# Six of 32 softmax tiles from ScalarE to VectorE: exponential from integer bits, summed in three terms by the PV matmuls

## The chip, the cores and the metric

The kernel runs on one core of a Trainium2 chip. The metric is device time in microseconds; every figure called a time is the median of several executions. The engines are called by their names or by the profile's short forms: PE is TensorE (PEld its weight loads), ACT is ScalarE, DVE is VectorE, POOL is GpSimd, SP issues most DMAs. "Clock" is the share of TensorE's full clock that was granted.

## The reference

```python
x = A_x                                        # 1 x 2048 x 512, bf16
xn = layernorm(x)
out = x + attention(xn, wqkv, wo) + mixer(xn, w1, b1, w2, b2)

def attention(x, wqkv, wo):                    # H = 32 heads, Dh = 16
    q, k, v = split(x @ wqkv)
    p = softmax(q @ k.T * Dh ** -0.5)          # 32 heads of 2048 x 2048
    return (p @ v) @ wo

def mixer(x, w1, b1, w2, b2):                  # an MLP over the 2048 tokens, F = 1376
    h = layernorm(x)
    return (gelu(h^T @ w1 + b1) @ w2 + b2)^T
```

There are 32 x 2048 x 2048 exponentials, 134 million. That is what makes this kernel a ScalarE kernel: in its trace ScalarE is busy 97% of the span, 946.2 of 953.8 us with them.

## The kernel before

The attention is cut into 32 blocks (four query blocks of 512 by eight groups of four heads). A block has 16 "periods", one for each 128 keys. In a period PE makes the scores of four heads (four matmuls of K = 32, in four row strips of the array), ScalarE turns them into exponentials as two tiles of 128 x 1024, and two periods later PE multiplies them with V (four matmuls in four column strips, 0.40 us for the four, accumulating in one PSUM bank for the whole block). V has a column of ones, so its 17th output row is the softmax denominator. Scores have three slots of two PSUM banks each.

```python
def pslot(n):                                   # tile n uses slot n % 3
    return n % 2 if n < 2 * NKT else n % 3

def score_group(g, rs=(0, 1, 2, 3)):
    ...
    for r in rs:
        n = 2 * g + r // 2
        bk = 2 * pslot(n) + (r % 2)
        matmul(bank(bk), lhsT=KT[32*r:32*r+32, T, 128*kt:128*(kt+1)],
               rhs=QT[32*r:32*r+32, slot_q, :], tile_position=(32*r, 0))

def exp_pair(n):
    activation(pT[:, n % NPB, :], ps[:, s_*1024:(s_+1)*1024], ACTF.Exp, scale=0.25)

def pv_group(g):
    ...
    for r in range(4):                          # accumulates over kt = 0..15
        matmul(bank(PV_BANK)[32*r:32*r+32, :], lhsT=V17[:, off:off+32],
               rhs=pT[:, buf, 512*(r%2):512*(r%2+1)], tile_position=(0, 32*r))

def task_epilogue_rest(b):                      # DVE: denominators, 4 reciprocals of 128x128
    stream_shuffle(denb, OT32, [16] * 32)
    for c in range(4): reciprocal(denb[:, cs], denb[:, cs])
    gpsimd.tensor_tensor(oT, OT32, denb, mult)
```

The main loop fixes the order in which every engine gets its instructions; each engine has its own list, and the timelines show it worked through in order (in e9_inter, which has another order on PE, a PV pass starts at 782.37 us, between the score pairs at 782.05 and 782.70). In a period PE gets the four score matmuls, the PV matmuls that are due, and then up to two "side" matmuls (projections of later blocks, the MLP, the output projection), which share one bank:

```python
while True:                                     # one turn is one period
    ...
    score_group(period); exp_pair(2*period); exp_pair(2*period + 1)
    pv_group(period - LAG)                      # when due; block end: epilogue
    ...                                         # side work: at most EXTRA_BUDGET = 2 matmuls
```

The softmax here doesn't subtract the row's maximum and nothing guards it: scores larger than these inputs give would overflow.

Of the kernel before, what the change touches and what calls it, by code (L numbers as in the profile page):

```python
# [9 lines left out]
BF16 = mybir.dt.bfloat16  # L10
F32 = mybir.dt.float32
# [3 lines left out]
H = 32  # L15
# [7 lines left out]
NKT = 16  # L23
# [5 lines left out]
DEBUG_SCHED = False  # L29
LAG = 2  # L30
NPB = 10
NQS = 3
EXTRA_BUDGET = 2.0
NW1 = 2
# [150 lines left out]
def bass_parallel_sum__softmax_full_mha__mixer_token_mlp__prompt_kernel(  # L185
# [18 lines left out]
    with ExitStack() as es:  # L204
# [23 lines left out]
        pT = sb("pT", [128, NPB, 1024], BF16)  # L228
        OT32 = sb("OT32", [128, 2, 512], F32)
# [4 lines left out]
        w2blk = sb("w2blk", [128, NW2, NFT, 128], BF16)  # L234
# [5 lines left out]
        stats = sb("stats", [128, 2 * NT, 6], F32)  # L240
        mv = sb("mv", [128, 2 * NT, 4], F32)
# [3 lines left out]
        osb = sb("osb", [128, 2, 512], BF16)  # L245
        ps = es.enter_context(nc.psum_tensor("ps", [128, 8 * 512], F32))
# [37 lines left out]
        sc.add("dve", lambda e: e.memset(v17_main[:, :, 16:17], 1.0), writes=[("Vone",)])  # L284

        sc.add("pool", lambda e: e.memset(qmask[:, 0:1], 0.0), writes=[("qmask",)])
        for r in range(4):
            sc.add("pool", lambda e, r=r: e.memset(qmask[32 * r:32 * r + 16, 0:1], 1.0),
                   reads=[("qmask",)], writes=[("qmask",)])
        sc.add("pool", lambda e: e.tensor_scalar(qmask[:, 1:2], qmask[:, 0:1], -1.0, 1.0, ALU.mult, ALU.add),  # L290
# [46 lines left out]
        def ln_stats(t, which):  # L337
            src = x_sb if which == 0 else xn_sb
            skey = ("x", t) if which == 0 else ("xn", t)
            i = which * NT + t  # L340
            sc.add("dve", lambda e: e.bn_stats(stats[:, i, :], src[:, t, :]),  # L341
                   reads=[skey], writes=[("stats", i)])
            sc.add("dve", lambda e: e.bn_aggr(mv[:, i, 0:2], stats[:, i, :]),
                   reads=[("stats", i)], writes=[("mv", i)])
            sc.add("pool", lambda e: e.tensor_scalar(mv[:, i, 1:2], mv[:, i, 1:2], EPS, None, ALU.add),
                   reads=[("mv", i)], writes=[("mv", i)])
            sc.add("pool", lambda e: e.tensor_tensor(mv[:, i, 2:3], mv[:, i, 1:2], mhalf[:], ALU.pow),  # L347
                   reads=[("mv", i), ("mhalf",)], writes=[("mv", i)])

        def ln_norm(t, which):  # L350
            src = x_sb if which == 0 else xn_sb
            dst = xn_sb if which == 0 else h_sb
            skey = ("x", t) if which == 0 else ("xn", t)
            dkey = ("xn", t) if which == 0 else ("h", t)
            i = which * NT + t
            sc.add("dve", lambda e: e.tensor_scalar(dst[:, t, :], src[:, t, :], mv[:, i, 0:1], mv[:, i, 2:3],
                                                    ALU.subtract, ALU.mult),
                   reads=[skey, ("mv", i)], writes=[dkey])

        def ln_tile(t, which):  # L360
            ln_stats(t, which)
            ln_norm(t, which)
# [88 lines left out]
        def vT_evac(tiles, T, bk, evac_eng):  # L451
            n = len(tiles)
            t0_ = tiles[0]
            assert tiles == list(range(t0_, t0_ + n))
            dst = V17[:, t0_ * H * 17:(t0_ + n) * H * 17].rearrange("p (t h c) -> p t h c", t=n, c=17)[:, :, 8 * T:8 * T + 8, 0:16]
            src = bank(bk)[:, 0:128 * n].rearrange("p (t h d) -> p t h d", t=n, d=16)
            evac(evac_eng, dst, src, reads=[("bank", bk)], writes=[("V", t, T) for t in tiles])

# [14 lines left out]
        def pro_stage(s_, pre):  # L473
# [24 lines left out]
            if 0 <= t < NT and (t < NPRE + 2 or not pre):  # L498
                ln_stats(t, 0)
            t = s_ - 1  # L500
            if 0 <= t < NT and (t < NPRE + 2 or not pre):
                ln_norm(t, 0)
# [25 lines left out]
        def pro_stage_late(s_):  # L528
# [17 lines left out]
            if NPRE + 2 <= t < NT:  # L546
                ln_stats(t, 0)
            t = s_ - 1
            if NPRE + 2 <= t < NT:
                ln_norm(t, 0)  # L550

        def task_ln2():
            for t in range(NT):
                yield 0.0
                ln_stats(t, 1)
                yield 0.0
                ln_norm(t, 1)
                yield 0.0
# [32 lines left out]
        def task_w2_load(st):  # L591
# [3 lines left out]
                reads=[], writes=[("w2blk", slot)], name="ld_w2a")  # L595
            dma("sp", w2blk[0:F - 128 * (NFT - 1), slot, NFT - 1, :],
                B_w2[128 * (NFT - 1):F, 128 * st:128 * (st + 1)],
                reads=[], writes=[("w2blk", slot)], name="ld_w2b")
# [28 lines left out]
        def task_yt(st):  # L627
            slot = st % NW2
            for ft in range(NFT):
# [5 lines left out]
                    reads=[("w2blk", slot), ("gT", ft)], writes=[("bank", EX_BANK)])  # L635
# [27 lines left out]
        def final_store(st, bk):  # L663
            ob = st % 2
            sc.add("dve", lambda e: e.tensor_tensor(osb[:, ob, :], bank(bk), resid[:, st, :], ALU.add),  # L665
# [25 lines left out]
        def task_epilogue_rest(b):  # L691
            qb, G = divmod(b, NG)
            eb = b % 2
            yield 0.0
            sc.add("dve", lambda e: e.stream_shuffle(denb[:, eb, :], OT32[:, eb, :], [16] * 32),  # L695
                   reads=[("OT32", eb)], writes=[("denb", eb, c) for c in range(4)])
            for c in range(4):
                cs = slice(128 * c, 128 * (c + 1))
                yield 0.0
                sc.add("dve", lambda e, cs=cs: e.reciprocal(denb[:, eb, cs], denb[:, eb, cs]),  # L700
                       reads=[("denb", eb, c)], writes=[("denb", eb, c)])
            yield 0.0
            sc.add("pool", lambda e: e.tensor_tensor(oT[:, qb % 2, G, :], OT32[:, eb, :], denb[:, eb, :], ALU.mult),  # L703
                   reads=[("OT32", eb)] + [("denb", eb, c) for c in range(4)],
# [49 lines left out]
        def exp_pair(n):  # L754
            s_ = pslot(n)
            buf = n % NPB
            sc.add("act", lambda e: e.activation(pT[:, buf, :], ps[:, s_ * 1024:(s_ + 1) * 1024], ACTF.Exp, scale=0.25),  # L757
                   reads=[("bank", 2 * s_), ("bank", 2 * s_ + 1)], writes=[("pT", buf)], name="exp")

        def pv_group(g):  # L760
            b, kt, qb, G, T, e_ = blk_of(g)
            for r in range(4):
                n = 2 * g + r // 2
                buf = n % NPB
                h = 8 * T + 2 * r + e_
                off = (kt * H + h) * 17
                sc.add("pe", lambda e, r=r, buf=buf, off=off: e.matmul(  # L767
                    bank(PV_BANK)[32 * r:32 * r + 32, :], lhsT=V17[:, off:off + 32],
                    rhs=pT[:, buf, 512 * (r % 2):512 * (r % 2 + 1)],
                    start=(kt == 0), stop=(kt == NKT - 1), tile_position=(0, 32 * r)),  # L770
                    reads=[("V", kt, T), ("pT", buf), ("Vone",)] + (
                        [("V", kt, T + 1)] if T < 3 else ([("V", kt + 1, 0)] if kt + 1 < NKT else [("Vpad",)])),
                    writes=[("bank", PV_BANK)], name="pv")
# [16 lines left out]
        for ft in range(NFT):  # L790
            sched_list.append((P(4, 2) + 6 * ft, 2, "ut", ft))
        for st in range(NT):
            sched_list.append((P(4, 2) + 6 * NFT + 7 * st, 3, "yt", st))
        for qb in range(NQB):
            for sti in range(4):
                if qb < NQB - 1:
                    sched_list.append((P(8 * (qb + 1) + 6, 2) + 4 * sti, 0, "op", (qb, sti)))
                else:
                    sched_list.append((P(NBLK - 2, 8) + 5 * sti, 4, "op", (qb, sti)))
# [33 lines left out]
        END = NGRP + LAG + 1  # L833
        while True:
# [9 lines left out]
            if period == P(7, 0):  # L844
                for st in range(min(NW2, NT)):
                    task_w2_load(st)
                w2_loaded = min(NW2, NT)
            if period < NKT:
                score_group(period, (0, 1))
                exp_pair(2 * period)  # L850
                score_group(period, (2, 3))
                exp_pair(2 * period + 1)
            elif period < NGRP:
                score_group(period)
                exp_pair(2 * period)
                exp_pair(2 * period + 1)
            for gp in (period - LAG - 1, period - LAG):
                if not (0 <= gp < NGRP):
                    continue
                b, kt = divmod(gp, NKT)  # L860
                due = gp + LAG + (1 if (kt == 0 and b > 0) else 0)
                if due != period:
                    continue
                pv_group(gp)
                if kt == NKT - 1:
                    if b == NBLK - 1:
                        assert sl_idx >= len(sched_list) and not any(tk.kind == "op" for tk in bank_q), \
                            "pre-accumulation of the last q block must be complete before the tail"
                        tail_epilogue(b)
                    else:  # L870
                        epilogue_copy(b)
                        free_tasks.append(Task("epi", b, task_epilogue_rest(b)))
# [14 lines left out]
            while bank_q:  # L887
                tk = bank_q[0]
                if tk.req is None:
                    bank_q.pop(0)  # L890
                    if DEBUG_SCHED:
                        print("period", period, "blk", period // NKT, "done", tk.kind, tk.arg)
                    if tk.kind == "ut" and w1_loaded < NFT:
                        task_w1_load(w1_loaded)
                        w1_loaded += 1
                    if tk.kind == "yt" and w2_loaded < NT:
# [82 lines left out]
```

## Time and profile before

| | before |
|---|---|
| time, median | 983.94 us (3 runs, 980.77 to 985.01) |
| span of the profiled run | 979.6 us |
| ScalarE busy | 953.8 us (97%) |
| of that in 1024 exponentials | 946.2 us |
| steady distance from start to start of two exponentials | 903 ns |
| VectorE busy | 306.4 us (31%) |
| TensorE: mean clock | 0.81 |

The first lines of the page of the kernel before give each engine's busy time, share of the span and number of instructions; in the row of the clock each digit is one of 40 slices of the span, in tenths of the full clock.

```profile
PE 822.8 (84%) x5019; PEld 208.2 (21%) x5084; DVE 306.4 (31%) x522; ACT 953.8 (97%) x1045; POOL 70.1 (7%) x110
...
PEclk9999859988878888999999999555955555555797
```

PE looks nearly as busy as ACT, but its matmul ends are modelled, and part of its time is pacing by the exponentials. The chain of waits of the same kernel (shares of the span, by engine and then by line) says who is followed:

```profile
ACT 87%; PE 10%; DVE 2%; issue 1%; DMA 1%; ACTq 0%; SPq 0%; DVEq 0%
ACT pT L757 86%; PE ps L748 3%; PE ps L767 2%; PE ps L605 1%; PE ps L425 1%; DMA x_sb<-in_A_x_dram 1%; ACT ga_sb L620 1%; PE ps L389 0%; PE ps L407 0%; DVE denb L717 0%; PE ps L652 0%; DVE QT L438 0%; PE ps L445 0%; DVE osb L665 0%; DVE sta
```

The groups of instructions of the kernel before show what fills ScalarE, and that PE's score matmuls (line 748) sat 102.1 us waiting for the exponentials (line 757) that free their PSUM slots. The columns are line, engine, operation, tiles, shapes and count, then busy time, mean duration of one, and the idle time before, with its cause.

```profile
L757 ACT ACTIVATE pT<-ps 128x1024 bf16<-128x1024 f32 x1024 | 946.2, 1390 | 4.2 <-PE ps L748 2.6
L748 PE MATMUL ps<-QT,KT 32*128 32x512 bf16 x2048 | 448.9, 464 | 123.5 <-ACT pT L757 102.1
...
L700 DVE RECIPROCAL denb<-denb 128x128 f32<-128x128 f32 x124 | 108.8, 920 | 0.9
```

The mean duration of 1390 ns is no cost: neighbouring activations overlap. What counts is the distance from start to start in the trace: 903 ns at the median, and also at its 25th and 75th percentile. One stretch of the timeline of the kernel before (start, length, what) has 34 exponentials in 31.8 us without a gap:

```profile
start us, us, engine line op out<-in xcount [idle before <-releaser]
854.20 31.81 ACT L757 ACTIVATE pT<-ps 128x1024 bf16<-128x1024 f32 x34
```

### The profile page before, as it was taken

What the parts mean: (1) busy time and instruction counts of PE and PEld (TensorE: products, weight loads), DVE (VectorE), ACT (ScalarE), POOL (GpSimd) and SP (SyncE); (2) the same over time, 40 slices, a digit from 0 to 9 for tenths busy, and PEclk for the clock granted to TensorE, in tenths of its full rate; (3) what the DMA queues carried; (4) which work ended last, traced back from release to release, by engine and by line L of the source; (5) the groups of instructions that cost most, each with busy time, mean ns of one, the idle gap of its engine ahead of it and who ended that gap; (6) DMA issues with size and microseconds to landing.
All of it is one profiled execution on the core that took longest, in us unless ns stands there. A gap on an engine that the chain in (4) does not pass through costs nothing.

```text
span 979.6 us, 11965 instructions
## 1 busy us (share of the span) xinstructions
PE 822.8 (84%) x5019; PEld 208.2 (21%) x5084; DVE 306.4 (31%) x522; ACT 953.8 (97%) x1045; POOL 70.1 (7%) x110
## 2 busy tenths in 40 slices
PE   5888898787888878888888888989889898998885
PEld 3422213211111112222222222111211111111121
DVE  6666633234322343222333223122211212102233
ACT  5999999999999999999999999999999999999995
POOL 3213200000000000000000000000000000000000
PEclk9999859988878888999999999555955555555797
DMA  8000000122111100111011010000000000000000
GB/s 193 2 1 17 6 1 2 22 51 43 21 22 22 22 17 1 30 28 27 11 30 44 17 42 2 0 1 4 19 1 1 1 1 0 1 1 1 11 11 22
DMA packets 57013, 18.34 MB, mean 19 GB/s; under 512 B 50816, under 2 KB 56960, under 8 KB 56960
## 3 DMA queue, kind: packets, MB, share of 16 engines
q1 hardware_dynamic: 53792, 16.00, 7.1%
q10 hardware_dynamic: 3168, 1.57, 0.6%
q8 instruction: 40, 0.66, 0.3%
q14 instruction: 13, 0.11, 0.0%
HBM read 15.47 MB, written 2.10 MB: 18 GB/s over the span
## 4 chain that ended last, share of the span: by engine, by line
ACT 87%; PE 10%; DVE 2%; issue 1%; DMA 1%; ACTq 0%; SPq 0%; DVEq 0%
ACT pT L757 86%; PE ps L748 3%; PE ps L767 2%; PE ps L605 1%; PE ps L425 1%; DMA x_sb<-in_A_x_dram 1%; ACT ga_sb L620 1%; PE ps L389 0%; PE ps L407 0%; DVE denb L717 0%; PE ps L652 0%; DVE QT L438 0%; PE ps L445 0%; DVE osb L665 0%; DVE stats L341 0%
## 5 line engine op out<-in xcount | busy, mean ns | idle before, releaser
L757 ACT ACTIVATE pT<-ps 128x1024 bf16<-128x1024 f32 x1024 | 946.2, 1390 | 4.2 <-PE ps L748 2.6
L748 PE MATMUL ps<-QT,KT 32*128 32x512 bf16 x2048 | 448.9, 464 | 123.5 <-ACT pT L757 102.1
L767 PE MATMUL ps<-pT,V 128*32 128x512 bf16 x2048 | 240.3, 469 | 0.6 <-ACT pT L757 0.6
L748 PEld LDWEIGHTS ps<-QT,KT 32*128 32x128 bf16 x2048 | 95.3, 94 | 505.8 <-ACT pT L757 481.5
L688 DVE COPY OT<-ps 128x512 f32<-128x512 f32 x31 | 21.4, 692 | 322.0 <-PE ps L767 322.0
L700 DVE RECIPROCAL denb<-denb 128x128 f32<-128x128 f32 x124 | 108.8, 920 | 0.9
L703 POOL TENSOR_TENSOR oT<-OT,denb 128x512 bf16<-128x512 f32 x31 | 39.3, 1266 | 791.3 <-DVE denb L700 791.3
L767 PEld LDWEIGHTS ps<-pT,V 128*32 128x32 bf16 x2048 | 51.9, 97 | 148.1 <-issue 145.8
L605 PE MATMUL ps<-big,w1blk 128*128 128x512 bf16 (+1 forms) x158 | 54.5, 419 | 6.5 <-issue 3.6
L632 PE MATMUL ps<-gT,w2blk 128*128 128x512 bf16 (+1 forms) x160 | 53.0, 398 | 2.8 <-issue 1.8
L637 DVE SCALAR_TENSOR_TENSOR big<-ps,x_sb 128x512 f32<-128x512 f32 x16 | 11.1, 691 | 102.3 <-PE ps L632 102.3
L652 PE MATMUL ps<-wo_pad,oT 128*128 128x512 bf16 x107 | 35.5, 406 | 2.4 <-issue 1.7
L610 DVE TENSOR_SCALAR u_sb<-ps,b1col 128x512 f32<-128x512 f32 (+1 forms) x11 | 8.3, 751 | 74.3 <-PE ps L605 74.3
L438 DVE TENSOR_SCALAR QT<-ps,qmask 128x512 bf16<-128x512 f32 x30 | 21.1, 747 | 32.3 <-PE ps L425 32.3
L665 DVE TENSOR_TENSOR osb<-ps,big 128x512 bf16<-128x512 f32 x16 | 11.0, 688 | 52.1 <-PE ps L652 52.0
L425 PE MATMUL ps<-xnT,wqkv_sb 128*128 128x512 bf16 x49 | 21.4, 509 | 2.6 <-issue 2.6
L695 DVE STREAM_SHUFFLE denb<-OT 128x512 f32<-128x512 f32 x31 | 22.4, 721 | 0.0
L415 DVE CAST V<-ps 128x128 bf16<-128x128 f32 (+1 forms) x26 | 12.4, 477 | 22.8 <-PE ps L569 22.2
L347 POOL TENSOR_TENSOR mv<-mv,mhalf 128x1 f32<-128x1 f32 x32 | 18.2, 567 | 2.7
L407 PE MATMUL ps<-xnT,wqkv_sb 128*128 128x512 bf16 x42 | 14.7, 423 | 2.7 <-DVE KT L415 1.6
L605 PEld LDWEIGHTS ps<-big,w1blk 128*128 128x128 bf16 (+1 forms) x176 | 10.7, 101 | 28.4 <-issue 24.4
L415 DVE CAST KT<-ps 128x128 bf16<-128x128 f32 (+1 forms) x26 | 12.2, 469 | 14.4 <-PE ps L407 9.1
(59 smaller groups left out, 211.8 us busy)
## 6 DMA issues: line engine op xcount, KB each, us to landing
w1blk<-in_B_w_dram SPq DMA_DIRECT2D x10, 512.0 KB, 4.1
w2blk<-in_B_w_dram SPq DMA_DIRECT2D x16, 320.0 KB, 3.3
out_dram<-osb SPq DMA_DIRECT2D x16, 128.0 KB, 1.7
x_sb<-in_A_x_dram SPq DMA_DIRECT2D x3, 512.0 KB, 9.9
wqkv_sb<-in_A_wqkv_dram ACTq DMA_DIRECT2D x3, 384.0 KB, 11.2
wo_pad<-in_A_wo_dram SPq DMA_DIRECT2D x8, 64.0 KB, 2.0
wqkv_sb<-in_A_wqkv_dram ACTq DMA_DIRECT2D x3, 128.0 KB, 3.8
w2blk<-in_B_w_dram SPq DMA_DIRECT2D x16, 24.0 KB, 1.7
```

The costliest lines, as they stand in the source:

```text
L415: return sc.add("dve", lambda e: e.tensor_copy(dst, src), reads=reads, writes=writes)
L425: sc.add("pe", lambda e, ct=ct: e.matmul(bank(bk), lhsT=wqkv_sb[:, ct, 128 * T:128 * (T + 1)], rhs=xnT[:, ct, 512 * qb:512 * (qb + 1)], st ...
L605: sc.add("pe", lambda e, st=st: e.matmul(bank(EX_BANK)[0:m, :], lhsT=w1blk[:, slot, st, 0:m], rhs=h_sb[:, st, :], start=(st == 0), stop=(s ...
L632: sc.add("pe", lambda e, ft=ft, m=m: e.matmul(bank(EX_BANK), lhsT=w2blk[0:m, slot, ft, :], rhs=gT[0:m, ft, :], start=(ft == 0), stop=(ft = ...
L652: sc.add("pe", lambda e, G=G: e.matmul(bank(EX_BANK), lhsT=oT[:, par, G, 128 * sti:128 * (sti + 1)], rhs=wo_pad[:, G, :], start=(G == 0), ...
L688: sc.add("dve", lambda e: e.tensor_copy(OT32[:, eb, :], bank(PV_BANK)), reads=[("bank", PV_BANK)], writes=[("OT32", eb)])
L695: sc.add("dve", lambda e: e.stream_shuffle(denb[:, eb, :], OT32[:, eb, :], [16] * 32), reads=[("OT32", eb)], writes=[("denb", eb, c) for c ...
L700: sc.add("dve", lambda e, cs=cs: e.reciprocal(denb[:, eb, cs], denb[:, eb, cs]), reads=[("denb", eb, c)], writes=[("denb", eb, c)])
L703: sc.add("pool", lambda e: e.tensor_tensor(oT[:, qb % 2, G, :], OT32[:, eb, :], denb[:, eb, :], ALU.mult), reads=[("OT32", eb)] + [("denb" ...
L748: sc.add("pe", lambda e, r=r, bk=bk: e.matmul(bank(bk), lhsT=KT[32 * r:32 * r + 32, T, 128 * kt:128 * (kt + 1)], rhs=QT[32 * r:32 * r + 32 ...
L757: sc.add("act", lambda e: e.activation(pT[:, buf, :], ps[:, s_ * 1024:(s_ + 1) * 1024], ACTF.Exp, scale=0.25), reads=[("bank", 2 * s_), (" ...
L767: sc.add("pe", lambda e, r=r, buf=buf, off=off: e.matmul(bank(PV_BANK)[32 * r:32 * r + 32, :], lhsT=V17[:, off:off + 32], rhs=pT[:, buf, 5 ...
```

## The change

ScalarE is full (busy 97%) and VectorE two thirds idle (busy 31%), so six of the 32 tiles of each block (from block 1 on: 186 of 1024) go to VectorE. The kernel uses no exponential instruction there; it builds the exponential from bits. The queries are scaled so that a score is 128 x log2 of its exponential. Add 16256 (127 x 128), convert to int16, and read the 16 bits as bf16: the exponent field is the integer part e and the mantissa field the fraction f, that is W = 2^e (1 + f). With A = 2^e (mantissa masked off) and M = W x (1 + f)^2, the sum W + A + (171/1024) M is close to 2.167 x 2^(e+f) for all f. The three terms are not added on VectorE: the PV matmul is run three times, with W and A against V and with M against a copy of V scaled by 171/1024. ScalarE's exponentials must carry the same factor 2.167, and get it as a bias of ln 2.167, a per-partition operand `kap`.

The rest of the change makes room for this. The denominators no longer go through a shuffle and four wide reciprocals, but by DMA into a compact 128 x 16 tile, one small reciprocal, and back by DMA. The product with them moves from GpSimd to VectorE. The statistics of the second layer norm are computed from those of the first, and the MLP's two weights share buffers. Side work is spaced further apart. The core of the diff, cut:

```diff
+QSCALE = 128.0 * 1.4426950408889634 * 0.25
+LN2_128 = 0.6931471805599453 / 128.0
+LNKAPPA = 0.773366911
+CM = 171.0 / 1024.0
+IBIAS = 16256.0
+DPOS = (2, 7, 12, 17, 22, 27)
 LAG = 2
+LAGD = 4
-NPB = 10
+NPB = 9
+NDB = 2
 ...
-            sc.add("act", lambda e: e.activation(pT[:, buf, :], ps[...], ACTF.Exp, scale=0.25), ...)
+            sc.add("act", lambda e: e.activation(pT[:, buf, :], ps[...], ACTF.Exp,
+                                                 bias=kap[:], scale=LN2_128), ...)
+        def exp_dve(n):
+            ...
+            tensor_scalar(dW_i[:, buf, :], ps[...], IBIAS, 0.0, ALU.add, ALU.max)       # PSUM -> int16
+            tensor_scalar(dm1_i, dW_i[:, buf, :], 0x7f, 0x3f80, bitwise_and, bitwise_or)
+            yield                                                                       # next period
+            tensor_scalar(dA_i[:, buf, :], dW_i[:, buf, :], -128, None, bitwise_and)
+            tensor_tensor(dm1, dm1, dm1, mult)
+            yield
+            tensor_tensor(dM[:, buf, :], dW[:, buf, :], dm1, mult)
+        def pv_seq(b):
+            for g in range(b * NKT, (b + 1) * NKT):
+                ns = [n for n in (2 * g, 2 * g + 1) if not is_d(n)]
+                if ns:
+                    steps.append([g + LAG, [(n, "P") for n in ns]])
+                for n in (2 * g, 2 * g + 1):
+                    if is_d(n):
+                        steps.append([g + LAGD, [(n, "W")]])
+                        steps.append([g + LAGD, [(n, "A")]])
+                        steps.append([g + LAGD, [(n, "M")]])
 ...
-            sc.add("dve", stream_shuffle ...)  # and 4 reciprocals, product on GpSimd
+            for r in range(4): dma("sp", dcomp[32*r:32*r+32, eb, :], OT32[32*r+16:32*r+17, eb, :] ...)
+            for _ in range(EPI_W1): yield 0.0
+            reciprocal(rcomp[:, eb, :], dcomp[:, eb, :])
+            dma("sp", rden_d[eb] ..., rcomp[:, eb, :]); 4 x dma("sp", denb[...], rden_d ... broadcast)
+            for _ in range(EPI_W2): yield 0.0
+            sc.add("dve", tensor_tensor(oT[...], OT32[:, eb, :], denb[:, eb, :], mult))
```

## The prediction

It was made from the text of both kernels and the profile of the kernel before.

VectorE's five steps came to about 3.3 us a tile and 19.9 us a block. Of their terms the read of PSUM is about 1225 ns, an estimate that continues the line from 291 ns for 128 elements to 692 ns for 512, both in the profile of the kernel before. The same terms are in VectorE's 22 to 27 us a block and its 820 us, and so in the total of 872 us, from which 870 was forecast. The 990 ns for ScalarE are 903 ns and the 90 ns between the 687 and 597 that the prediction quotes. In the last paragraph the first of the conditions is cut.

> **What bounds it now.** ScalarE. The engine table gives ACT 953.8 us busy of 979.6 (97%). The groups table puts 946.2 us of that in 1024 exponentials of 128x1024, and the chain of waits gives 86% of the span to them. Their steady start-to-start distance in the timeline is 903 ns. VectorE is busy 306 us (31%). PE shows 84%, much of it pacing: its score matmuls waited 102 us for exponentials. Block 0 ends near 47 us; the other 31 blocks take 28.9 to 30.7 us each.
>
> **What the change removes.** 6 x 31 = 186 exponentials leave ScalarE: 186 x 0.903 = 168 us. From VectorE go 124 reciprocals (108.8 us), 31 shuffles (22.4), the second LN's statistics (10.8 + about 3).
>
> **What it adds.**
> VectorE, per moved exponential, five instructions. Trace durations: PSUM fp32 reads of 512 take 692 ns, so one of 1024 about 1225; a bf16 SBUF tensor-scalar of 512 takes 382, [...]. Independent neighbours overlap by 80 to 90 ns in the timeline, so about 3.3 us each, 19.9 us a block. With its other work: 22 us a block late, 25 to 27 early. VectorE's busy time should rise to about 820 us.
> PE: four more PV matmuls per moved tile (744), At full clock a step costs about 0.11 us to switch plus 0.215 us per pass: 1.1 us per group of four heads without side work, 1.5 to 1.6 us with it.
> ScalarE: the bias becomes a per-partition operand. The existing exponential has an isolated duration of 1018 ns and shows no such cost; the one activation with a per-partition scale does (687 ns at 512 against 597). [...] If not hidden, the distance becomes about 990 ns and returns 75 of the 168 us. I think that likely.
>
> **On the critical path.** ScalarE per block: 26 x 0.903 to 0.99 = 23.5 to 25.8 us, plus tanh. VectorE: 22 to 27. PE: 18 to 26. So first VectorE and PE limit, later ScalarE. Three PSUM slots and in-order queues couple them, so I add some 3% stalls. Sum: 47 (block 0) + 6 x 27.5 + 8 x 27 + 8 x 26 + 9 x 25.5 + tail 6 = 872 us. The denominators' DMA exchange should stay off the path. PE's granted clock should mostly stay at 1.0: it was 0.5 only in the late stage with few matmuls per window (about 220), and these become denser.
>
> **Predicted:** 870 us, 8 in 10 between 835 and 908. Faster by over 2%: 0.96; within 2%: 0.03; slower: 0.01.
>
> **Right or wrong would show as:** exponential start-to-start 0.90 or 0.99 us; ACT busy share falling to about 90 to 95%; VectorE near 820 us busy (94%); ACT's idle put down to score matmuls which waited for VectorE's first step; last-stage clock near 1.0.
>
> **What would make it wrong:** [...] PE at half clock, where a block would need over 30 us; denominators landing late, which stalls VectorE in order; or a hidden bias cost and little coupling (830 to 845).

## More of the kernel before

From block 1 on, all distances together exceed 903 ns by 24 us. That is all that ScalarE waited, or spent on other things, in 920 us.

Between 600 and 930 us the clock is at one half for most of the time (263 us), and hardly anything is lost: the distances exceed 903 ns by only 7 us there. A period of two exponentials lasts 1.8 us, and PE's work kept to it even at half clock: in the timeline PV passes of four start at 800.21 and 802.04 us, 1.83 us apart.

## The result, and the profile after

| | before | after |
|---|---|---|
| time, median | 984.47 us (4 runs) | 949.50 us (4 runs, 943.86 to 951.69) |
| span of the profiled run | 979.6 us | 949.7 us |
| exponentials on ScalarE, steady distance | 1024, 903 ns | 838, 996 ns |
| distances over the steady one, from block 1 on | 24 us | 87 us |
| ScalarE / VectorE busy | 953.8 / 306.4 us | 868.3 / 778.2 us |
| TensorE at half clock (clock records, which run 2 us past the span) | 381 us | 154 us |

The ratio is 0.964 (95% interval 0.961 to 0.968). Ratios here and below are the mean time of one kernel's fast runs over that of the other's fast runs of the same rounds, so not quite the ratio of the medians quoted.

The kernel became faster, but by 3.6% where 11.6% was forecast, and 949.5 us lies outside the range of 835 to 908. The page of the changed kernel, the same lines as before:

```profile
PE 806.3 (85%) x5752; PEld 237.4 (25%) x5828; DVE 778.2 (82%) x1296; ACT 868.3 (91%) x859; POOL 35.5 (4%) x78
...
PEclk9989999987888989799999999998999889878898
```

The chain is no longer ScalarE's alone. PE holds a third of it and VectorE a fifth:

```profile
ACT 43%; PE 34%; DVE 20%; issue 2%; DMA 1%; SPq 0%; ACTq 0%; POOL 0%; DVEq 0%
ACT pT L828 42%; PE ps L853 15%; PE ps L805 11%; DVE dW L837 7%; PE ps L654 3%; PE ps L681 2%; DVE dM L849 2%; DVE dm L846 1%; DVE QT L479 1%; DVE dm L840 1%; PE ps L466 1%; DVE KT L456 1%; PE ps L618 1%; DVE u_sb L659 1%; DVE ga_sb L662 1%
```

The groups of the changed kernel: line 828 is the exponential, 805 the scores, 837 to 849 the five VectorE steps, 853 the PV matmuls.

```profile
L828 ACT ACTIVATE pT<-ps,kap 128x1024 bf16<-128x1024 f32 x838 | 857.6, 1138 | 57.9 <-PE ps L805 55.1
L805 PE MATMUL ps<-QT,KT 32*128 32x512 bf16 x2048 | 328.6, 409 | 104.7 <-ACT pT L828 69.1
L837 DVE TENSOR_SCALAR dW<-ps 128x1024 int16<-128x1024 f32 x186 | 227.0, 1221 | 106.7 <-PE ps L805 105.4
...
L849 DVE TENSOR_TENSOR dM<-dW,dm 128x1024 bf16<-128x1024 bf16 x186 | 128.0, 688 | 4.2
L846 DVE TENSOR_TENSOR dm<-dm 128x1024 bf16<-128x1024 bf16 x186 | 127.2, 684 | 0.0
...
L840 DVE TENSOR_SCALAR dm<-dW 128x1024 int16<-128x1024 int16 x186 | 80.4, 432 | 6.4
...
L844 DVE TENSOR_SCALAR dA<-dW 128x1024 int16<-128x1024 int16 x186 | 76.2, 410 | 0.0
```

Three readings follow. First, the five VectorE steps are as cheap as forecast: 1221, 432, 410, 684 and 688 ns. The first had been put at 1225. The five add up to 3.44 us without overlaps; 3.3 had been written, with overlaps of 80 to 90 ns taken off. Second, 838 exponentials take 857.6 us, so each takes longer than before. The trace's view of the tile `kap`, ScalarE's part (duration in ns, minimum, median, maximum), has its fastest at 1093 ns; the same view of `pT` in the kernel before had 1018. First the kernel before:

```profile
L757 ACT ACTIVATE pT<-ps x1024: 1018/1338/2016, 15.8 to 966.4; 128x1024 bf16<-128x1024 f32 x171
```

And the changed kernel's:

```profile
L828 ACT ACTIVATE pT<-ps,kap x838: 1093/1123/1300, 15.2 to 937.5; 128x1024 bf16<-128x1024 f32 x168
```

The steady start-to-start distance rose from 903 to 996 ns. Third, ScalarE idled 57.9 us before exponentials, 55.1 of them until a score matmul was done: PE, not VectorE directly, came late. The score matmuls themselves waited longer for ScalarE to free a slot than for VectorE's first step. The view of waits (who waited for whom, us in total, times, longest):

```profile
PE ps L805 <- ACT pT L828: 69.1, 168, 1.6
PE ps L805 <- DVE dW L837: 29.4, 42, 2.7
```

This gives a sum that closes to 2 us. Moving 186 exponentials saves 186 x 0.903 = 168 us. The longer distance of those left costs 838 x 0.093 = 78 us. Waits rise from 24 to 87 us, 62 us. That leaves 28 us; the profiled spans differ by 29.9. The sum closes because waits are defined as the remainder of the distances; it sizes the parts and does not explain the waits. Some 10 of the 87 us, and 6 of the 24, lie around ScalarE's 11 steps of the MLP's tanh.

How much ScalarE gets done goes with PE's clock; whether it depends on it, e3_fill below tests. Two windows of 49 us of the changed kernel (busy time and number of instructions for each engine in order, then clock, DMA share and GB/s): at full clock it does 48 activations, about what 996 ns allow, and at a mean clock of 0.79 it does 42.

```profile
196.00:245.00 49.00, 40.89 (x248) 9.91 (x248) 37.10 (x60) 41.24 (x42) 0.00 (x0) 0.79 0.18 39
441.00:490.00 49.00, 43.43 (x313) 12.32 (x314) 43.41 (x71) 48.18 (x48) 0.00 (x0) 1.00 0.17 36
```

The timeline of the changed kernel shows such a moment. At 855.10 four PV passes that are due in one period begin (W, A and M of a VectorE tile, and the tile from ScalarE). The first starts at full clock, then the clock halves, starts come 0.4 us apart instead of 0.2, and the next score matmuls do not start before 856.73 (PE's matmuls alone):

```profile
855.10 0.41 PE L853 MATMUL ps<-dW,V 128*32 128x512 bf16 x2
855.33 0.61 PE L853 MATMUL ps<-dA,V 128*32 128x512 bf16 x2
855.73 0.64 PE L853 MATMUL ps<-dM,VM 128*32 128x512 bf16 x2
856.16 0.64 PE L853 MATMUL ps<-pT,V 128*32 128x512 bf16 x2
856.73 0.67 PE L805 MATMUL ps<-QT,KT 32*128 32x512 bf16 x4
```

### The profile page after: what moved, and what is told of

It reads as the page before. It is cut to its first block, busy times and chain, and to the rows that moved or that the text cites. A ratio compares the mean times of both kernels' runs of the same rounds, so it can differ in the third digit from the quotient of the medians.

```text
span 949.7 us, 14370 instructions
## 1 busy us (share of the span) xinstructions
PE 806.3 (85%) x5752; PEld 237.4 (25%) x5828; DVE 778.2 (82%) x1296; ACT 868.3 (91%) x859; POOL 35.5 (4%) x78
## 4 chain that ended last, share of the span: by engine, by line
ACT 43%; PE 34%; DVE 20%; issue 2%; DMA 1%; SPq 0%; ACTq 0%; POOL 0%; DVEq 0%
ACT pT L828 42%; PE ps L853 15%; PE ps L805 11%; DVE dW L837 7%; PE ps L654 3%; PE ps L681 2%; DVE dM L849 2%; DVE dm L846 1%; DVE QT L479 1%; DVE dm L840 1%; PE ps L466 1%; DVE KT L456 1%; PE ps L618 1%; DVE u_sb L659 1%; DVE ga_sb L662 1%
## 5 line engine op out<-in xcount | busy, mean ns | idle before, releaser
L828 ACT ACTIVATE pT<-ps,kap 128x1024 bf16<-128x1024 f32 x838 | 857.6, 1138 | 57.9 <-PE ps L805 55.1
L805 PE MATMUL ps<-QT,KT 32*128 32x512 bf16 x2048 | 328.6, 409 | 104.7 <-ACT pT L828 69.1
L837 DVE TENSOR_SCALAR dW<-ps 128x1024 int16<-128x1024 f32 x186 | 227.0, 1221 | 106.7 <-PE ps L805 105.4
L849 DVE TENSOR_TENSOR dM<-dW,dm 128x1024 bf16<-128x1024 bf16 x186 | 128.0, 688 | 4.2
L846 DVE TENSOR_TENSOR dm<-dm 128x1024 bf16<-128x1024 bf16 x186 | 127.2, 684 | 0.0
L840 DVE TENSOR_SCALAR dm<-dW 128x1024 int16<-128x1024 int16 x186 | 80.4, 432 | 6.4
L853 PE MATMUL ps<-dM,VM 128*32 128x512 bf16 x372 | 79.0, 421 | 0.0
L853 PE MATMUL ps<-dW,V 128*32 128x512 bf16 x372 | 78.6, 419 | 0.0
L853 PE MATMUL ps<-dA,V 128*32 128x512 bf16 x372 | 78.2, 417 | 0.0
L844 DVE TENSOR_SCALAR dA<-dW 128x1024 int16<-128x1024 int16 x186 | 76.2, 410 | 0.0
```

The source lines that it names most:

```text
L805: sc.add("pe", lambda e, r=r, bk=bk: e.matmul(bank(bk), lhsT=KT[32 * r:32 * r + 32, T, 128 * kt:128 * (kt + 1)], rhs=QT[32 * r:32 * r + 32 ...
L828: sc.add("act", lambda e: e.activation(pT[:, buf, :], ps[:, s_ * 1024:(s_ + 1) * 1024], ACTF.Exp, bias=kap[:], scale=LN2_128), reads=[("ba ...
L837: sc.add("dve", lambda e: e.tensor_scalar(dW_i[:, buf, :], ps[:, s_ * 1024:(s_ + 1) * 1024], IBIAS, 0.0, ALU.add, ALU.max), reads=[("bank" ...
L840: sc.add("dve", lambda e: e.tensor_scalar(dm1_i[:], dW_i[:, buf, :], 0x7f, 0x3f80, ALU.bitwise_and, ALU.bitwise_or), reads=[("dW", buf)], ...
L844: sc.add("dve", lambda e: e.tensor_scalar(dA_i[:, buf, :], dW_i[:, buf, :], -128, None, ALU.bitwise_and), reads=[("dW", buf)], writes=[("d ...
L846: sc.add("dve", lambda e: e.tensor_tensor(dm1[:], dm1[:], dm1[:], ALU.mult), reads=[("dm1",)], writes=[("dm1",)], name="dm2")
```

## The experiments

Every kernel ran beside the kernel before on the same chip, in three rounds. The sets ran on different chips (e1 to e4 and e13 to e16 on one, e5 to e8 on another, e9 to e12, e17 and e18 on a third). The kernel before had medians of 981.8 to 984.9 us in all of them, so medians of different sets are compared where it helps, and a few microseconds between sets mean nothing. "Waits" are, as above, what ScalarE's start-to-start distances exceed their steady value by, from block 1 on. The kernels of the runs "fill", "five", "four", "short" and "paired" build on one another; what they start from is said each time.

### The bias operand: e1_nobias, e2_before_bias

Theory A: the per-partition bias costs 93 ns per exponential (996 less 903) and this is on the path. Rival B: PE and VectorE set the pace, and it is hidden. The first kernel needs no bias: the factor 2.167 is taken out of VectorE's integers instead of put into ScalarE's exponentials.

```diff
-IBIAS = 16256.0
+IBIAS = 16256.0 - 128.0 * 1.4426950408889634 * LNKAPPA
-            e.activation(..., ACTF.Exp, bias=kap[:], scale=LN2_128)
+            e.activation(..., ACTF.Exp, scale=LN2_128)
```

> The changed kernel without the per-partition bias: the factor 2.167 is taken out of VectorE's integer offset instead (16256 minus 142.8), so results stay correct. Theory A (the bias operand costs ScalarE 93 ns per exponential and ScalarE is on the path whenever PE runs at full clock): distance of exponentials back to 903 ns, ScalarE busy near 790 us, time 895 to 910 us. Rival B (PE and VectorE set the pace and the bias is hidden behind them): distance back to 903 ns where unwaited, but time 935 us or more, with ScalarE idle over 140 us.

Measured: 906.03 us, correct, ratio 0.921 (0.917 to 0.924). The most frequent distance is back at 903 ns (the median, with more waits in it, is 919). That is 43.5 us less than 949.5, for two changed lines. The time lies inside theory A's 895 to 910; what it frees is not all 78 us, because waits grew to 121 us by the same count.

The second kernel is the kernel before with nothing but the bias added:

```diff
+        sc.add("pool", lambda e: e.memset(kap[:], 0.773366911), writes=[("kap",)])
-            e.activation(..., ACTF.Exp, scale=0.25)
+            e.activation(..., ACTF.Exp, bias=kap[:], scale=0.25)
```

> The kernel before, with a constant per-partition bias in its exponential and nothing else changed (the common factor cancels in the softmax, results correct). Theory A: 996 ns between exponentials, 1024 x 93 ns = 95 us longer, so 1072 to 1082 us. Rival (the longer distance in the changed kernel comes from VectorE reading PSUM at the same time, not from the operand): under 1000 us.

Measured: 1067.31 us, correct, ratio 1.085 (1.082 to 1.088), distance 996 ns. It is 82 us longer, and 5 us below the forecast range; 8 us of ScalarE's waits disappeared in the longer periods. No VectorE work on the scores is in this kernel, so the rival, that VectorE's reading of PSUM slows ScalarE, is out. The group of exponentials in e2_before_bias:

```profile
L759 ACT ACTIVATE pT<-ps,kap 128x1024 bf16<-128x1024 f32 x1024 | 1032.9, 1365 | 3.2 <-PE ps L750 3.1
```

The same group in e1_nobias:

```profile
L828 ACT ACTIVATE pT<-ps 128x1024 bf16<-128x1024 f32 x838 | 790.5, 1044 | 79.6 <-PE ps L805 75.8
```

1024 exponentials with the operand take 1032.9 us against 946.2; 838 without it take 790.5 us against 857.6.

### PE's clock: e3_fill, e4_nobias_fill

Theory C: the drops to half clock make ScalarE wait. In the changed kernel's trace fewer matmuls start per us in the half-clock stretches than at full clock (4.6 against 6.3, counted from 49 to 900 us; a few records can be missing). Whether PE's having less to do brings the drops is not shown by that, so the test gives it more: in a period with neither side matmuls nor a VectorE tile's passes, two more PV passes with a weight tile of zeros, which change nothing in the sum.

```diff
+            if NKT <= period < NGRP and <no side matmul in this period> and 0 < pv_i < len(pv_steps):
+                for _ in range(0 if d_now else 2):
+                    for r in range(4):
+                        matmul(bank(PV_BANK)[32*r:32*r+32, :], lhsT=zw[:], rhs=pT[:, buf, ...],
+                               start=False, stop=False, tile_position=(0, 32*r))
```

> The changed kernel with two passes of four zero-weight PV matmuls in every group of four heads that has neither MLP or projection matmuls nor a VectorE tile's PV passes; results correct. Theory C (the drops of PE's clock to one half, 154 us of the profiled run, cost about 39 us of ScalarE waits): mean clock over 0.97 and 915 to 930 us. Rival D (drops are harmless; the waits come from VectorE and PE's order): clock up, time within 6 us of 949.5, or longer because the fillers take PE's time.

Measured: 925.27 us, correct, ratio 0.940 (0.936 to 0.944), mean clock 0.979. Matmuls that compute nothing made the kernel 24 us faster. Time at half clock fell from 154 to 41 us. ScalarE's waits in such stretches fell from 39 to 8 us, those at full clock stayed (47 and 50 us). The row of the clock with fillers, to be held against that of the changed kernel above:

```profile
PEclk9989999999899999899999999999999999999998
```

> No bias operand and the fillers together; results correct. A and C together: 862 to 880 us, clock over 0.97. A without C: as e1_nobias, within 6 us. B and D: 930 us or more.

Measured: 896.10 us, correct, ratio 0.910 (0.907 to 0.914). Both together give 53 us, and less than 43.5 + 24.2: each hides part of the other. The forecast of 862 to 880 was a miss. At 903 ns ScalarE no longer limits even at full clock, and 98 us of waits remain there. The chain of e4_nobias_fill:

```profile
PE 42%; DVE 31%; ACT 21%; issue 2%; DMA 2%; SPq 1%; ACTq 0%; DVEq 0%
```

### How many tiles: e5_five, e6_four

```diff
-DPOS = (2, 7, 12, 17, 22, 27)
+DPOS = (2, 9, 14, 21, 26)        # e5_five     (3, 10, 19, 26) in e6_four
```

Both start from e4_nobias_fill.

> No bias operand, fillers, and five tiles of 32 on VectorE instead of six (positions 2, 9, 14, 21, 26); results correct. Theory E (with the bias gone, VectorE's chain holding a PSUM slot late, and PE's extra passes, are what still makes ScalarE wait about 98 us at full clock): waits fall by more than the 31 x 0.9 = 28 us of exponentials that come back, so 872 to 888 us against 896. Rival (the waits come from the MLP and projection work, whatever the count): 28 us more exponentials on the path, 915 to 925 us.

> The same with four tiles of 32 (positions 3, 10, 19, 26); results correct. Theory E: waits nearly gone, ScalarE at 28 x 0.903 = 25.3 us a block again the limit, 860 to 885 us. Rival: 940 us or more.

Measured: 894.51 us (ratio 0.910) and 921.37 us (0.938), both correct. Theory E half fell. Six and five are equal; with four, 62 exponentials (56 us) come back to ScalarE, and its waits fall only to 76 us where they should have been nearly gone (109 with six tiles, 79 with five). In e6_four they stand in four places of the block, 14 to 17 us at each, summed over all blocks: at tiles 4, 12, 20 and 28, always the first tile of the next period after one with a VectorE tile (3, 10, 19, 26).

The trace shows what meets there. The passes W, A and M of a tile come four periods after it (LAGD), and the four positions of e6_four, in periods 1, 5, 9 and 13, are four periods apart, so that every period with a VectorE tile also has the three passes of the one before. ScalarE has a single exponential, 0.9 us, to cover them, while PE takes 1.83 us (median) from the second score pair of such a period to the next scores, against 1.18 to 1.19 in most periods without such passes. One such period in the timeline of e6_four, from its second score pair to the next scores and ScalarE's late exponential (lines between left out):

```profile
646.64 0.39 PE L807 MATMUL ps<-QT,KT 32*128 32x512 bf16 x2 [0.36 <-ACT pT L830]
646.96 0.39 PE L855 MATMUL ps<-dW,V 128*32 128x512 bf16 x2
647.62 0.38 PE L855 MATMUL ps<-pT,V 128*32 128x512 bf16 x2
648.47 0.40 PE L807 MATMUL ps<-QT,KT 32*128 32x512 bf16 x4
648.90 1.94 ACT L830 ACTIVATE pT<-ps 128x1024 bf16<-128x1024 f32 x2 [0.48 <-PE ps L807]
```

With six or five tiles the two meet only once in a block, before tile 4, where ScalarE waits 16 us in e4 and e5 and 17 us in e6, again summed over all blocks. In e5_five 63 of the 79 us stand at tiles 4, 12, 18, 24 and 30, each the first after a period with three such passes. So e6_four changed the arrangement together with the number. It does not show that the waits are independent of the number, and four tiles at other positions were not run.

### VectorE's chain or PE's passes: e7_dve_short, e8_pe_short, e13_both_short

These start from e4_nobias_fill and leave out work. In e7 VectorE makes W only, and all three PV terms read it; in e8 VectorE makes everything, and PE sums W only; e13 has both cuts.

```diff
 # e7_dve_short: the four steps after dexp are dropped
-            src, key = {"W": (dW, "dW"), "A": (dA, "dA"), "M": (dM, "dM")}[term]
+            src, key = dW, "dW"
 # e8_pe_short
-                        steps.append([g + LAGD, [(n, "A")]])
-                        steps.append([g + LAGD, [(n, "M")]])
```

> Wrong result on purpose. No bias operand, fillers, six tiles; VectorE does only the first step of each tile and all three PV terms read its output, so PE's work is unchanged and VectorE loses about 410 us. If VectorE's chain is the remaining limit: 820 to 845 us. If PE's extra passes are: 880 us or more.

> Wrong result on purpose. No bias operand, fillers, six tiles; VectorE's chain complete, but PE sums only the first of the three terms (744 matmuls fewer). If PE's extra passes are the remaining limit: 830 to 855 us. If VectorE's chain is: 880 us or more.

> Wrong result on purpose. No bias operand, fillers, six tiles; VectorE does one step per tile and PE sums one pass per tile, both cuts together. If VectorE's chain and PE's extra passes each cause their own part of the remaining waits (28 and 30 us when cut alone): 836 to 848 us. If either cut alone had opened the same waits: 858 to 866 us.

Measured: 867.77, 866.13 and 828.00 us (ratios 0.883, 0.882, 0.842). e8 and e13 are wrong (relative error 0.134). e7 still passed the comparison: 2.167 W is the exponential with straight lines between powers of two, and the tolerance lets it through; it is not the same function, and was meant as a probe. VectorE's chain is worth 28 us and PE's passes 30 us; both together 68. With VectorE's steps cut PE holds 46% of the chain of waits, with PE's passes cut VectorE 41%. Both forecasts of a single cause fell, and so did e13's range, on the fast side: the parts are separate and help each other. With both cut, ScalarE is the limit again. The chain of e13_both_short:

```profile
ACT 62%; PE 27%; DVE 8%; issue 1%; DMA 1%; SPq 0%; ACTq 0%; DVEq 0%
```

### Another order on PE: e9_inter, e10_inter_only, e11_inter_nobias, e12_inter_five

Theory F was that PE's in-order list is the trouble: with a tile of the period on VectorE, ScalarE has one exponential (0.9 us) to cover all the PV passes and side matmuls that stand in front of the next scores. So the PV passes were put between the two score pairs of a period (e9 on e4_nobias_fill, e10 on the changed kernel, e11 on e1_nobias, e12 on e5_five).

```diff
-            if period < NGRP:
-                for i in range(2):
-                    <two score matmuls, one exponential>
-            while pv_block < NBLK: <PV passes that are due>
+            for i in range(2):
+                if period < NGRP: <two score matmuls, one exponential>
+                while pv_block < NBLK and i == (0 if period >= NKT else 1): <PV passes that are due>
```

> No bias operand, fillers, six tiles, and in every group of four heads PE's PV passes are issued between the two pairs of score matmuls instead of behind both; results correct. Theory F (PE's in-order queue: with a tile of a group on VectorE, ScalarE has one exponential, 0.9 us, to cover all of the group's PV passes and side matmuls, about 1.5 us, which stand in front of the next score matmuls; hence the waits at positions 4, 16 and 26, just after three extra passes): those waits, 49 of 102 us, go mostly away, so 850 to 872 us against 896. Rival G (VectorE releases PSUM slots late; the order on PE is harmless): within 8 us of 896.

> The changed kernel with that order of issue alone (bias operand kept, no fillers); results correct. F: the waits at positions 4, 16 and 26, 41 of 79 us, go mostly away: 910 to 928 us against 949.5. G: within 8 us of 949.5.

> That order and no bias operand, no fillers; results correct. F: 858 to 882 us against 906. If the fillers still matter, 8 to 15 us above e9_inter; if closing the waits keeps PE dense enough, within 5 us of it.

> As e9_inter with five tiles of 32; results correct. F: with the waits gone ScalarE's count decides, so it becomes slower than e9_inter or equal: 860 to 880 us. G: within 8 us of 894.5.

Measured: 942.21, 982.81, 954.18 and 914.53 us, all correct; ratios 0.957, no verdict, 0.970 and 0.932. All four are slower than without the reorder: by 46 us (e9 against e4), 48 (e11 against e1) and 20 (e12 against e5). One of e9's four runs was slow. For e10 only one run was fast (967.58 us, 18 us above 949.5); it has no ratio. The edit did not test F, because it changed something else. The timeline of e9_inter shows it: a lone pass of two or four matmuls is followed by the next kind only 0.32 us later.

```profile
782.05 0.39 PE L807 MATMUL ps<-QT,KT 32*128 32x512 bf16 x2
...
782.37 0.40 PE L855 MATMUL ps<-pT,V 128*32 128x512 bf16 x4
...
782.70 0.39 PE L807 MATMUL ps<-QT,KT 32*128 32x512 bf16 x2
...
783.02 0.61 PE L703 MATMUL ps<-wo_pad,oT 128*128 128x512 bf16 x2
783.13 1.94 ACT L830 ACTIVATE pT<-ps 128x1024 bf16<-128x1024 f32 x2 [0.48 <-PE ps L807]
...
783.56 0.39 PE L807 MATMUL ps<-QT,KT 32*128 32x512 bf16 x2
...
783.88 0.39 PE L855 MATMUL ps<-dW,V 128*32 128x512 bf16 x2
```

Over the trace of the changed kernel, at full clock, start to start takes 216 ns between PV passes of one kind, and 317 ns from a score pass to a PV pass, 315 back. A change of kind costs 0.10 us. From block 1 on e4 has about 1310 changes, e9 about 1855; and score pairs that ran as one pass of four now run apart (some 750 score passes against 930). At 216 ns for a pass and 102 more for a change, an estimate from these numbers, PE needs about 85% of the time from block 1 on in e4 and about 93% in e9. So the edit filled PE up; that this made it slower is argued. Theory F itself was not tested; the trace of e6_four above agrees with it.

### The other parts: e14_five_w6, e15_six_w6, e16_none

```diff
-EPI_W1 = 3
+EPI_W1 = 6           # e14 (on e5_five), e15 (on e4_nobias_fill)
-D_FIRST_BLOCK = 1
+D_FIRST_BLOCK = 99   # e16, on e1_nobias: no tile on VectorE at all
```

> No bias operand, fillers, five tiles, and three periods more between the start of the denominators' transfer and the reciprocal that reads it; results correct. In the run with five tiles VectorE stood 32 us waiting for that transfer (26 times). If that wait is on the path: 878 to 889 us against 894.5. If VectorE has room there: 892 to 897 us.

> The same for six tiles, where VectorE waited only 4 us: 891 to 898 us, no change against 896.

> Everything else of the change (denominators by DMA, second LN from the first, scaled queries, spacing of the side work) but no tile on VectorE and no bias operand; results correct. If the rest is neutral for the time: 976 to 988 us, exponentials 903 ns apart. If the denominators or the spacing cost by themselves: 995 us or more.

Measured: 911.45, 903.67 and 988.04 us, all correct (ratios 0.927, 0.920, 1.005). More time for the denominators' transfer made it worse, by 17 and 8 us. The wait that it aimed at did go: VectorE waited 32 us for the transfer in with five tiles and not at all in e14. But it then stood once, in block 2, for the transfer back, 5.9 us in e14 and 10.0 in e15. The timelines show why: SyncE takes 15 us there to issue eight loads of the output weights (`wo_pad`). In e4 the reciprocal's DMA goes out at 85.6 us, before these loads; in e15 the reciprocal is done at 94.7 us, just after they began, and its DMA goes out behind them at 108.6. ScalarE's one wait of 11.7 us that follows in e15 is more than its 8 us; in e14 the same event cost it 5.6 us of the 17, and the rest was not found out. e16 shows that the rest of the change, the compact denominators, the second LN and the wider spacing, brings no gain by itself: 1.005 (1.003 to 1.008). There VectorE waited 54 us for the transfer in and 60 us for the transfer back, and had room for it.

### Fewer passes, same matmuls: e17_paired, e18_paired_nofill

The W, A and M of an even tile use two column strips and those of an odd tile the other two. If the even one waits for the odd one, three passes of four serve both (in e17 the 372 matmuls on W take 38.3 us of PE in all, in e4 74.2). e17 starts from e4_nobias_fill, e18 from e1_nobias.

```diff
-                        steps.append([g + LAGD, [(n, "W")]])   # and A, M: three passes for each tile
+                        i = DPOS.index(n % (2 * NKT))
+                        if i % 2:
+                            n0 = n - DPOS[i] + DPOS[i - 1]
+                            for term in "WAM":
+                                steps.append([g + LAGD, [(n0, term), (n, term)]])
-NDB = 2
+NDB = 3              # for dW and dA; NPB 9 -> 8 pays for it
```

> No bias operand, fillers, six tiles; the PV passes of two VectorE tiles, one of heads 0 and 1 and one of heads 2 and 3, are issued together, so three passes of four matmuls serve two tiles (9 passes fewer in a block, the same matmuls); three buffers for two of VectorE's outputs and one fewer for the exponentials; results correct. If PE's passes as such are the cause of their 30 us: 866 to 880 us against 896. If it was the number of matmuls, or the clock: 890 to 900 us.

> The same without fillers; results correct. Against 906 us for no bias operand alone: 876 to 892 us if the passes are the cause; the clock will drop more often, since PE does less, so 5 to 15 us above e17_paired.

Measured: 887.07 us (ratio 0.904, 0.902 to 0.905) and 919.04 us (0.935), both correct. e17 is the fastest correct kernel (e7, a probe, left aside), 62 us under the change as made, but it gains 9 us where 16 to 30 were expected. It cuts nine of the twelve passes that e8 left out of each block and gains under a third of e8's 30 us, so fewer passes alone did not bring those. The pairing also delays the even tile's passes and takes one of nine buffers from the exponentials; no run separates that. Without fillers the paired version is 13 us slower than e1 and not faster: its clock fell to 0.88 (219 us at half clock against 97). With fillers the clock stays at 0.97 and the same pairing gains, so the loss without them goes with the clock.

## Why the prediction was wrong

**The direction and the first term were right.** 186 x 0.903 = 168 us left ScalarE, and the new VectorE steps cost about what had been forecast: 1221 ns for the PSUM read against 1225, and 3.44 us for a tile before overlaps against 3.3 after them. The bitwise steps took 432 and 410 ns and the products 684 and 688; the profile of the kernel before shows neither kind. VectorE's busy time was 778 us, not 820.

**The bias operand was seen, and then only half put into the sum.** The prediction named it ("If not hidden, the distance becomes about 990 ns and returns 75 of the 168 us. I think that likely"), and it came nearly so: 996 ns, 78 us. The kernel before had one activation with such an operand, 90 ns longer than one without (687 against 597 ns at 512 elements), and its exponentials overlap (mean duration 1390 ns, 903 from start to start). So it was open whether the overlap would swallow the cost; e2_before_bias shows that it does not (903 to 996 ns). But the forecast then did not add up: 984 - 168 + 78 is 894 us with no new wait at all, and 870 is 24 us below, as if all the old waits were to vanish too. The blocks were written down as 25.5 to 27.5 us where 26 x 0.996 alone is 25.9.

**The step that failed is "Three PSUM slots and in-order queues couple them, so I add some 3% stalls".** The mean block of the sum was (872 - 47 - 6) / 31 = 26.4 us, which leaves 0.5 us for waits above 25.9. The profile after has 87 us of waits in 31 blocks, 2.8 us each, about 10% of the time. The 31 blocks took 890 us where the sum had 819; block 0 (49 us against 47) and the tail (11 against 6) add 7. Experiments give what is in them: PE's drops to half clock are worth 24 us with the bias and 10 without (e3, e4); VectorE's chain and PE's extra passes 28 and 30 us each alone and 68 together (e7, e8, e13), measured without the bias and with fillers, so they are not a partition of the 87. That three engines, each busy 24 to 27 us in a block, give in order nearly 29 us, and not their maximum, is what the forecast missed.

**"PE's granted clock should mostly stay at 1.0" was wrong where it counted.** The clock did rise, from 0.81 to 0.92. But a half-clock stretch that cost little before (7 us of waits between 600 and 930 us, of which 263 us were at half clock), when PE had slack, now stopped the chain: 39 of the 87 us of waits fell in them. And half clock was not confined to the late stage even before, which had 99 us of it between 47 and 600 us. What sets the clock is not shown. Long gaps between matmuls were not needed for a drop: in the kernel before, two matmuls in succession never start more than 1.42 us apart in the 8 us before a drop or inside a half-clock stretch (the tail left out), and not more than 0.95 us in the three longest, of 54.6 us. What the runs show is that zero-weight passes raised the mean clock from 0.92 to 0.98 (e3), for 24 us, and that the paired kernel without fillers, with nine passes fewer in a block than e1, had 0.88 (e18) against e1's 0.95.

**"The denominators' DMA exchange should stay off the path" was right** for the kernel as changed (VectorE waited 2.7 us for it), as was "the bottleneck is shared".

What stays open: how much of the waits comes from the number of VectorE's tiles and how much from their arrangement over the periods; the exact division of the last 40 us or so above ScalarE's own time, even in e13; and two thirds of what e14 lost.

## What to carry to other kernels

When work is moved off a full engine, first price what the move does to the work that stays: here a bias operand took back 78 of 168 us, and a constant folded into the other side brought the distance back from 996 to 903 ns. When three engines end up near the same load, in order and with three slots between them, do not forecast the largest of the three; the measured loss was 10%, and shared waits show as each engine holding part of the chain. And look at whether a resource with slack, such as a half-clocked TensorE, keeps its slack after the change: here all waits between 600 and 930 us, 263 of them at half clock, came to 7 us before, and the waits at half clock to 39 us after.
